# The order and engine choice of all tasks in a fused attention and GLU kernel

## The chip, the cores and the metric

The kernel runs on one core of a Trainium2 chip. The metric is the device time of one execution in microseconds (us); smaller is better. Engines are TensorE (PE in the profile), VectorE (DVE), ScalarE (ACT), GpSimd (POOL) and SyncE (SP), which here issues the DMAs.

## What is computed

One block of a conditioned transformer over 2048 tokens of width 512, with bf16 inputs and output. Cut to what matters:

```python
mod = silu(c) @ w_mod            # six vectors sa, ca, ga, sb, cb, gb of 512
h = layernorm(x) * (1 + ca) + sa
q, k, v = h @ wqkv               # 32 heads of 16
phi(t) = concat(softmax(t @ w_phi), softmax(-(t @ w_phi)))   # 32 features a head
kv = sum over tokens of phi(k) x v;   z = sum over tokens of phi(k)
o = (phi(q) @ kv) / (phi(q) @ z + 1e-6)
x = x + ga * (o @ wo)
h = layernorm(x) * (1 + cb) + sb
x = x + gb * ((sigmoid(h @ w_gate) * (h @ w_up)) @ w_down)   # inner width 1376
```

No query can be finished before kv and z hold the sum over all tokens: that is the one place where everything meets.

## The kernel before

The tokens lie in 16 tiles of 128. The kernel is written as about a thousand named tasks, each with the engines that may run it, the values that it reads and writes, and the buffers that it holds. A string, `ORDER` (lines 39 to 87), lists all of them once, in one order for all engines; a name may carry the letter of its engine (`@A` ScalarE, `@D` VectorE, `@P` GpSimd), and without one it takes its first alternative. `Graph.arrange` walks the string, gives each task its engine and hands out buffer slots (eight banks of PSUM, and fixed numbers of slots for features, reciprocals and so on), first freed, first used. `emit` then issues the tasks in that order:

```python
for word in text.split():
    name, _, e = word.partition("@")
    t = self.tasks[name]
    t.eng = LETTER[e] if e else next(iter(t.alts))
...
def emit(order):
    for t in order:
        ...
        t.fn(t.eng)
```

So every engine, and SyncE's queue of DMAs, works through its own part of the string in that order, and waits where a value or a slot is not there yet. The string sets which task stands ahead of which on an engine, and nothing else in the file does.

The tasks, by stage, with the lines under which the profile shows them:

- Head: loads of x, weights and modulation vectors (L537 to L562), `warm` (L600: 6 + 12 matmuls on zeros, whose results nobody reads), `tpw`, `wTc`, `fold`, `foldc` (L661, 664, 679, 685: w_phi folded into the projections of q and k), the modulation's matmuls `modc` (L616, 630) with their copies (L635 to 638).
- For each tile the first normalization: `st1` (statistics, VectorE, L702/703), `rs1` (ScalarE L709/710 or GpSimd L712/713), `nmr1` (L718), `xn1` (L729, 731), transposes `tph` on TensorE (L744) or by DMA, `hm1` (scale and shift: L751 on ScalarE, L753 on VectorE or GpSimd).
- Features: matmuls `K` and `Q` (L817, 871), exponentials `e`, `qe` (ScalarE, L776), sums `n`, `qn` (VectorE, L780), reciprocals `r` (VectorE L798, ScalarE L794/795), products `phi` (L787) and `qphi` (L784) on VectorE or GpSimd; values `V` (L821) and their copy `va` (L836). `phi` and `qphi` have both of their inputs in SBUF. `pT` transposes a tile's qphi by a DMA (L874).
- `kv`: the sums over all tokens (L282) in two PSUM banks; `kvn`, `kvz` (L294, 299) mask them into `kvb` on VectorE, with `mask4` (L591).
- For each tile the attention's output: `num` (L326), `rd` (L329), `u` (L333), the transposition `oT`, `out` (L356), `x1` (L361), the second normalization `st2`, `rs2`, `nmr2`, `xn2` (L365 to L400), its transposition `xnT` (L407, 415) and `mod` (scale and shift: GpSimd L424, ScalarE L426, VectorE L422).
- The GLU in six chunks of 1, 1, 2, 4, 4 and 4 tiles: for each of 11 blocks of the inner width the matmuls `g` and `u` (L447, 449, 452), `tg` (ScalarE, L457), `hm` (VectorE, L468), and for each tile 11 matmuls `y` (L485) into one accumulator; `fin` (L492) adds x1 and `st` stores.
- A guard: `bnd` (L506 to L525) bounds the exponents from the folded weights (four reductions of 1024 columns on VectorE, then small steps) and sets a flag; a second, general path behind the main one is skipped if the bound holds.

Of the kernel before, what the change touches and what calls it, by code (L numbers as in the profile page):

```python
# [43 lines left out]
modc1c1 st1_8 ld_x3a warm1_8 K1a hm1_23 xn1_5 xn1_4 tph12 nmr1_6 st1_9 hm1_03@A hm1_13@A hm1_02@A ld_wv0 wqT3 xn1_10 xn1_11 rs1_5@P K0a K0b tph31 hm1_42@A
warm1_9 hm1_12@A hm1_22@A tph32 e0.0 K3a tph30 K3b hm1_30@A ld_wmga K1b tph33 warm1_10 tph40 st1_14 st1_15 st1_13 hm1_31@A hm1_32 wqT0 e3.0 wqT1 K2b hm1_40
nmr1_5 rs1_8@P n0.0 nmr1_8 hm1_33 e2.0 V0a V1a fold03 xn1_9 xn1_8 V1b V0b e1.0 n2.0 V2a V2b tph50 hm1_50 warm1_11 xn1_15 xn1_14 n1.0 V3a wqT2 fold00 fold01
tph43 r0.0@A va1 va0 phi0.0 foldc03 fold02 foldc01 foldc02 n3.0 st1_12 foldc00 xT1_10 xT1_11 r2.0 va2@D ld_wmm2 modca.0 modca.1 hm1_60@P hm1_63@P hm1_62@P
tph82 hm1_82@A r3.0@A modcac r1.0@A phi2.0@D phi1.0@D V3b K4a K4b rs1_7@P Q0 Q2 kv0.0 Q1 qe0.0 va3 qe2.0 hm1_43@A qe1.0 modc2.0 tph52 modc2.1 tph51 nmr1_7
xn1_12 xn1_13 phi3.0@D ld_wo qn0.0 modc2c e4.0 kv1.0 qn2.0 hm1_52 kv2.0 Q4 K5a kv3.0 xT1_12 xT1_13 qphi0.0@P qphi0.1@P qn1.0 qe4.0 qphi2.1 tph80 K5b hm1_80@A
hm1_51@A e5.0 pT0 qphi2.0 n4.0 r4.0@A qn4.0 n5.0 phi4.0@D qphi1.1@P hm1_61@P qphi1.0@P tph53 V5 K7a V4 va5 hm1_53@A V6 pT2 hm1_70@P qphi4.1 va4 hm1_71 mask4  # L50
va6 K6a K7b K6b e6.0 K8 tph83 hm1_83 r5.0 qphi4.0@P e8.0 pT1 pT4 ld_wd2 tph81 hm1_81 n6.0 n8.0 e7.0 n7.0 V7 kv4.0 hm1_72@P K11 K9 V9 K14 V8 r6.0@A e9.0 va7
va9 r7.0@A e11.2 e11.6 phi5.0 phi6.0 hm1_73@P n9.0 r9.0@A kv5.0 gwa gra gwb e11.4 e14.0 K10 phi7.0@D kv6.0 K12 V10 kv7.0 e14.4 r8.0 n11.6 n11.2 r11.6 phi9.0
e10.0 e12.0 ld_wd ld_wu0 grb n11.4 n14.0 r11.2 n14.4 r14.0 n10.0 r14.4@A phi8.0 va8 V11 V14 n12.0 e11.0 K13 n11.0 phi11.6 r11.4 wo1 r11.0 va10 r10.0@A va11
kv8.0 kv9.0 phi11.2@D phi11.0@D phi10.0@D phi11.4@D V12 K15 e13.0 wmod_free ld_wg0 phi14.4 phi14.0 kv10.0 kv11.4 kv11.6 Q6 kv11.0 e13.4 r12.0@A e15.4 n13.0
n13.4 r13.0 r13.4 n15.4 e15.0 va14 V15 V13 qe6.0 va12 kv11.2 n15.0 r15.0 r15.4@A va13 phi13.4 Q5 phi15.4 phi13.0@D va15 phi15.0@D phi12.0@D wo0 wo3 Q3 kv12.0
kv13.0 kv14.0 kv15.0 qn6.0 kvn0 kvz0 kv13.4 kv14.4 kv15.4 kvz1 kvn1 num0a num1a num2a wo2 rd0a wo_all rd1a qe3.0 u0a num0b num4a num1b rd0b Q11 qe5.0 rd2a u0b
u2a rd4a num2b qn3.0 u1a rd1b tpo0 Q8 qphi6.0@P qphi6.1@P oT0 out0 num4b rd2b u1b wd0 qe11.0 u2b qphi3.1@P qphi3.0@P x1_0 rd4b st2_0 qe8.0 Q7 qe7.0 tpo1 oT1
Q10 Q9 out1 Q15 oT2 rs2_0 qn5.0 nmr2_0 xn2_0 u4a u4b x1_1 qn7.0 tsw xnT0 out2 qphi5.1@P qphi5.0@P pT6 mod02 mod00 qphi7.0@P pT3 mod03@A mod01@A qe15.0
qphi7.1@P Q13 g0.8 x1_2 tg0.8 g0.1 st2_1 wd1 rs2_1 tg0.1 u0.8 u0.1 g0.0 num3b g0.4 hm0.1 hm0.8 pT5 qe9.0 tg0.4 g0.9 wd2 u0.4 u0.9 rd3b u3b tg0.9 g0.5 num3a
hm0.4 hm0.9 u0.2 u0.0 num6a tg0.5 tg0.0 rd3a u3a u0.5 g0.2 hm0.0 hm0.5 rd6a nmr2_1 qe10.0 tg0.2 oT4 g0.10 u0.10 wd6 hm0.2 g0.3 pT7 tg0.3 u6a g0.6 num6b u0.3  # L60
y0.0 y0.1 rd6b tg0.10 hm0.10 hm0.3 num5a num5b u6b rd5b wd3 wd4 wd5 oT3 oT6 xn2_1 qe13.0 tg0.6 rd5a y0.2 u5b g0.7 tg0.7 out4 u5a oT5 qn11.0 u0.6 u0.7 xnT1
num7a hm0.6 hm0.7 mod13@A mod12@A rd7a x1_4 y0.3 out3 qphi11.1@P qphi11.0@P x1_3 st2_3 out6 mod10@A mod11@A g1.2 tg1.2 g1.1 tg1.1 num7b wd7 u1.3 u1.2 hm1.2
u7a g1.4 u1.1 y0.4 rd7b hm1.1 u1.4 y0.5 tg1.4 hm1.4 g1.0 g1.10 u1.10 g1.3 u7b st2_2 rs2_2 tg1.10 tg1.3 hm1.10 hm1.3 pT11 out5 tg1.0 u1.7 g1.7 x1_6 nmr2_2 u1.0
hm1.0 g1.5 u1.5 x1_5 qn10.0 wd8 y0.6 g1.6 oT7 xn2_2 xn2_3 g1.8 y0.7 Q14 y0.8 wd10 tg1.7 tg1.5 hm1.5 out7 u1.8 u1.6 st2_4 tg1.6 xnT2 xnT3 wd9 x1_7 qphi10.0 Q12
hm1.7 st2_6 mod21@P mod20@P qphi10.1@P y1.0 pT10 tg1.8 mod22@A mod23@A hm1.6 g1.9 y1.1 y1.2 tg1.9 u1.9 y0.9 y1.3 y1.4 g2.5 y0.10 g2.6 st2_5 qe12.0 st2_7 hm1.8
qn9.0 tg2.5 qe14.0 rs2_4 hm1.9 rs2_3 nmr2_4 y1.5 u2.0 g2.1 g2.0 tg2.0 xn2_7@D hm2.0 nmr2_3 fin0 y1.6 g2.2 tg2.2 u2.6 u2.2 hm2.2 u2.1 num11b y1.7 g2.4 rd11b
u11b xn2_6@P xnT7 xnT6 u2.5 tg2.1 xn2_5 qphi9.1@P hm2.1 tg2.6 u2.8 xn2_4 hm2.5 g2.3 num11a rd11a u11a u2.9 qphi9.0@P xnT5 y1.8 xnT4 tg2.4 u2.4 hm2.4 hm2.6
tg2.3 g2.9 u2.3 hm2.3 g2.8 tg2.8 tg2.9 u2.7 mod41@P mod43@P mod32@P mod42@P mod31@P qn13.0 g2.10 hm2.8 g2.7 y1.9 num10a qn8.0 num10b y2.0 y1.10 tg2.7 hm2.7
rd10a hm2.9 qphi8.0@P u2.10 pT9 y2.1 y2.2 y2.3 y2.4 y2.5 qn14.0 num9b rd9b qphi13.0 qphi8.1@P mod30@A mod33@A tg2.10 mod40@A y2.6 y2.7 g3.3 wr qphi13.1@P
tg3.3 oT11 g3.0 u10a rd10b u10b pT8 oT10 hm2.10 qn15.0 g3.8 num9a rd9a u9a u3.0 out11 y2.8 g3.1 y2.9 qphi14.1 fin1 x1_11 u9b u3.3 hm3.3 st1 tg3.8 tg3.0 u3.8  # L70
num8a st2_11 num8b rd8b rd8a u8a pT13 qphi15.0 hm3.8 u8b u3.9 g3.4 u3.2 out10 x1_10 qphi14.0 oT8 oT9 hm3.0 st2_10 y2.10 g3.6 u3.6 qn12.0 rs2_6 out8 tg3.4
# [987 lines left out]
```

## Time and profile before

| | before |
|---|---|
| time, median of 3 runs | 205.47 us (205.26 to 205.93) |
| span of the profiled execution | 203.3 us |
| around the span (median less span) | 2.2 us |
| TensorE busy | 194.9 us, 96% of the span, 1447 matmul records |
| VectorE busy | 160.6 us, 79% |
| ScalarE busy | 105.9 us, 52% |
| GpSimd busy | 102.1 us, 50% |
| granted TensorE clock | 9 of 9 in each slice |
| DMA | 22.94 MB, mean 113 GB/s |

The profile's own execution has no separate time beside its span; the three timed runs stand 2.2 us above it. The page cuts the span in 40 slices and gives the busy share of each engine in tenths. A group of instructions stands with its count, its busy time and the mean of one, and with the idle time of the engine just before them and what ended it. In rows of the timeline the first number is the start, the second the length, and neighbours of one kind are one row.

### The profile page before, as it was taken

Reading aid. Unit: us, or ns where it says so; the run is one execution under the profiler, and the core shown is the slowest. Engines: PE = TensorE matmul, PEld = TensorE weight load, DVE = VectorE, ACT = ScalarE, POOL = GpSimd, SP = SyncE. Lnnn points to the kernel's source line nnn. Section 1 sums busy time; section 2 is a strip of 40 time slices with the busy share of each in tenths; the row PEclk is TensorE's granted clock in tenths of the full one; section 3 lists DMA queues with packets and bytes.
Section 4 is the critical chain, followed back from the end, with each engine's and each line's share of the span. In section 5 each row is a group of like instructions: output and inputs, shape, how many; then the busy total and the mean of one; then the engine's idle time right before and its main releaser. Section 6 shows DMA issues by size and latency. Waiting matters only on the chain.

```text
span 203.3 us, 4138 instructions
## 1 busy us (share of the span) xinstructions
PE 194.9 (96%) x1447; PEld 106.7 (52%) x1471; DVE 160.6 (79%) x374; ACT 105.9 (52%) x257; POOL 102.1 (50%) x143
## 2 busy tenths in 40 slices
PE   7789999999999999999999999999999999999993
PEld 2455655555464687668844444444444444444442
DVE  3899999999999999999897797794969844326633
ACT  2799999999978984556451115212113311324100
POOL 4698977789689999767670056230030324000000
PEclk9999999999999999999999999999999999999999
DMA  5999975669952792417637224433112030100111
GB/s 172 331 329 182 233 264 102 123 82 280 400 213 43 146 102 55 94 37 106 125 59 103 51 54 103 101 83 77 26 26 69 13 79 31 40 13 7 50 55 55
DMA packets 49453, 22.94 MB, mean 113 GB/s; under 512 B 38065, under 2 KB 47634, under 8 KB 49426
## 3 DMA queue, kind: packets, MB, share of 16 engines
q1 hardware_dynamic: 48896, 22.59, 48.6%
q8 instruction: 13, 0.21, 0.4%
q14 instruction: 14, 0.11, 0.2%
q10 hardware_dynamic: 530, 0.02, 0.1%
HBM read 11.58 MB, written 2.10 MB: 67 GB/s over the span
## 4 chain that ended last, share of the span: by engine, by line
PE 75%; DVE 8%; ACT 4%; DMA 4%; issue 4%; POOL 3%; SPq 0%; POOLq 0%; DVEq 0%
PE y_ps L485 19%; PE u_ps L447 18%; PE g_ps L447 17%; PE a_ps L356 5%; DMA wmod_sb<-in_w_mod_dram 4%; PE k_ps L817 3%; PE warm L600 3%; DVE ks L780 3%; PE num L326 2%; POOL phi L787 2%; PE q_ps L871 2%; PE v_ps L821 2%; PE g_ps L449 1%; ACT h1T L751 1%; DVE qks L780 1%
## 5 line engine op out<-in xcount | busy, mean ns | idle before, releaser
L457 ACT ACTIVATE tg<-g_ps 128x512 bf16<-128x512 f32 (+5 forms) x66 | 28.8, 455 | 66.7 <-PE g_ps L447 39.5
L468 DVE SCALAR_TENSOR_TENSOR wmod_sb<-tg,u_ps 128x512 bf16<-128x512 bf16 (+4 forms) x63 | 30.3, 492 | 18.0 <-ACT tg L457 11.3
L485 PE MATMUL y_ps<-wd_sb,wmod_sb 128*128 128x512 bf16 (+4 forms) x180 | 44.2, 366 | 0.2
L447 PEld LDWEIGHTS <-wg_sb 128*128 128x128 bf16 (+1 forms) x252 | 21.9, 99 | 16.1 <-issue 0.2
L447 PEld LDWEIGHTS <-wu_sb 128*128 128x128 bf16 (+1 forms) x252 | 21.8, 99 | 16.0 <-issue 0.3
L784 POOL TENSOR_TENSOR qphi<-qe,qks 128x512 bf16<-128x512 bf16 x24 | 25.1, 1063 | 3.9 <-DMA pT<-qphi 1.0
L485 PEld LDWEIGHTS <-wmod_sb 128*128 128x128 bf16 (+1 forms) x187 | 17.1, 98 | 16.0 <-issue 0.6
L447 PE MATMUL u_ps<-wT_sb,wu_sb 128*128 128x512 bf16 (+2 forms) x124 | 23.8, 322 | 0.1
L447 PE MATMUL g_ps<-wT_sb,wg_sb 128*128 128x512 bf16 (+2 forms) x122 | 23.0, 321 | 0.2
L447 PE MATMUL g_ps<-wqk_sb,wg_sb 128*128 128x128 bf16 (+4 forms) x127 | 19.9, 286 | 0.1
L447 PE MATMUL u_ps<-wqk_sb,wu_sb 128*128 128x128 bf16 (+4 forms) x127 | 19.8, 286 | 0.2
L492 DVE TENSOR_TENSOR ot<-y_ps,x 128x512 bf16<-128x512 f32 (+2 forms) x17 | 11.1, 654 | 10.5 <-PE y_ps L485 10.4
L780 DVE TENSOR_REDUCE qks<-qe 128x64 bf16<-128x1024 bf16 x16 | 19.2, 1204 | 0.0
L780 DVE TENSOR_REDUCE ks<-e 128x64 f32<-128x1024 bf16 (+2 forms) x22 | 19.1, 905 | 0.0
L376 POOL TENSOR_SCALAR ve<-mv 128x2 f32<-128x2 f32 (+1 forms) x8 | 1.8, 226 | 34.2 <-DVE mv L366 34.1
L776 ACT ACTIVATE e<-k_ps 128x512 bf16<-128x512 f32 (+2 forms) x44 | 17.7, 504 | 0.1
L776 ACT ACTIVATE qe<-q_ps 128x512 bf16<-128x512 f32 x32 | 17.3, 608 | 0.8 <-POOL phi L787 0.4
L787 POOL TENSOR_TENSOR phi<-e,kr 128x1024 bf16<-128x1024 bf16 (+2 forms) x10 | 14.5, 1454 | 3.9 <-ACT kr L795 2.1
L817 PE MATMUL k_ps<-wqk_f,h1T 128*128 128x512 bf16 x61 | 15.9, 379 | 0.1
L356 PE MATMUL a_ps<-wo_sb,oT 128*128 128x512 bf16 x60 | 15.9, 379 | 0.2
L871 PE MATMUL q_ps<-wqk_f,h1T 128*128 128x512 bf16 x60 | 15.7, 379 | 0.2
L821 PE MATMUL v_ps<-wv_sb,h1T 128*128 128x512 bf16 x62 | 15.5, 379 | 0.0
(131 smaller groups left out, 306.4 us busy)
## 6 DMA issues: line engine op xcount, KB each, us to landing
out_dram<-ot SPq DMA_DIRECT2D x15, 128.0 KB, 1.8
x_sb<-in_A_x_dram SPq DMA_DIRECT2D x6, 256.0 KB, 4.9
wmod_sb<-in_w_mod_dram SPq DMA_DIRECT2D x1, 1536.0 KB, 7.4
wu_sb<-in_B_w_up_dram SPq DMA_DIRECT2D x1, 1376.0 KB, 11.0
wg_sb<-in_B_w_gate_dram SPq DMA_DIRECT2D x1, 1376.0 KB, 10.4
wd_sb<-in_B_w_down_dram SPq DMA_DIRECT2D x1, 1280.0 KB, 8.0
wmod_sb<-in_w_mod_dram SPq DMA_DIRECT2D x4, 256.0 KB, 6.0
wqk_sb<-in_A_wqkv_dram SPq DMA_DIRECT2D x2, 256.0 KB, 4.5
```

What stands on the lines that cost most here:

```text
L356: pe.matmul(ap_[:], lhsT=oT[:, j, :], rhs=wo_sb[:, j, :], start=(j == 0), stop=(j == KT - 1))
L447: pe.matmul(ps[:fsz, 0:n], lhsT=w[:, j, ft * P:ft * P + fsz], rhs=h[:, j, 0:n], start=(j == 0), stop=(j == KT - 1))
L457: G.add(f"tg{k}.{ft}", {"ACT": 0.13 + n * 0.00083}, lambda e, tg=tg, g_ps=g_ps, fsz=fsz, n=n: act.activation(tg[:fsz, 0:n], g_ps[:fsz, 0:n ...
L468: dve.scalar_tensor_tensor(hm_all[:fsz, hm[k].slot, ft, 0:n], tg[:fsz, 0:n], 1.0, u_ps[:fsz, 0:n], op0=ALU.add, op1=ALU.mult)
L485: mm = pe.matmul(y[:, 0:c1 - c0], lhsT=hm_all[:fsz, hm[k].slot, ft, tl * P:(tl + 1) * P], rhs=wd_sb[:fsz, ft, c0:c1], start=(ft == 0), sto ...
L776: act.activation(ee[:, a:b, s].rearrange("p g f h -> p g (f h)"), kp[:, a * 64:b * 64].rearrange("p (g n) -> p g n", n=64), ACT.Exp, scale ...
L780: dve.tensor_reduce(ks[:, a:b].rearrange("p g s h -> p (g s) h"), ee[:, a:b].rearrange("p g s f h -> p (g s) h f"), axis=AX.X, op=ALU.add)
L784: engine(e).tensor_tensor(ph[:].rearrange("p (g s f h) -> p g s f h", s=2, f=DH, h=4)[:, :, s], ee[:, :, s], ks[:, :, 1 - s].unsqueeze(2). ...
L787: engine(e).tensor_tensor(ph[:, a * P:b * P].rearrange("p (g f h) -> p g f h", f=DH, h=4), ee[:, a:b].rearrange("p g s f h -> p (g s) f h" ...
L817: pe.matmul(kp[:], lhsT=h1T[:, j, t * P:(t + 1) * P], rhs=wqk_f[:, j, D:2 * D], start=(j == 0), stop=(j == KT - 1))
L821: pe.matmul(vp[:], lhsT=h1T[:, j, t * P:(t + 1) * P], rhs=wv_sb[:, j, :], start=(j == 0), stop=(j == KT - 1))
L871: pe.matmul(qp[:], lhsT=h1T[:, j, t * P:(t + 1) * P], rhs=wqk_f[:, j, 0:D], start=(j == 0), stop=(j == KT - 1))
```

## The change

Only `ORDER` changes, nearly everywhere. The tasks are the same: 1471 matmuls, the same loads and stores. Two lines of the diff, the first of the head (the others read alike):

```diff
 ORDER = """
-pmem ld_x0b wdz warm0 c1 warm1_0 warm1_1 bd st1_2 st1_3 warm1_2 warm1_3 c2 rs1_2 ld_x0a ld_wk0 warm1_4 tpw0 st1_0 rs1_0 wTc0 st1_1 ld_wk1 rs1_1 c3 xn1_0
...
+wdz warm0 c1 c2 warm1_0 warm1_1 warm1_2 warm1_3 ld_x0a mask4 st1_1 st1_0 rs1_0 warm1_4 ld_x0b st1_2 ld_wk0 ld_wk1 ld_x1b pmem bd st1_3 rs1_2@P tpw0 tpw1 rs1_1
...
```

55 tasks get another engine. Among them: the rs1 of tile 2 (ScalarE to GpSimd); one copy of the modulation, `modc1c1` (ScalarE to VectorE, L638); h1T of tile 3, `hm1_30` (ScalarE to VectorE) and `hm1_71` (ScalarE to GpSimd); the reciprocals r2, r5 and a quarter of r11 (VectorE to ScalarE), r9 and a half each of r14 and r15 (ScalarE to VectorE); a quarter of phi11 against another; of 32 halves of qphi VectorE runs 5 rather than 8 and GpSimd 27 rather than 24; of 36 modulations `mod` GpSimd runs 12 rather than 16, ScalarE 19 rather than 16 (in part L426 for L424).

Moved, by stage: all twelve single warming matmuls stand ahead of the first K, where four stood behind it. The second part of the modulation's matmuls (L616) stands behind K6 instead of ahead of K5. The loads of wo, wd, wu and wg stand behind the first pT in SyncE's queue (before, wo's was issued at 22.0 us, the others from 40.4 to 49.3). The y accumulators of chunks 3, 4 and 5 are opened four tiles at a time, with their y between the chunk's own g and u; the guard's reductions, the qphi of tiles 8 to 15 and the modulations of the third and fourth chunk stand earlier in the string.

The first place is VectorE ahead of and around the mask (L591, `mask4`: the mask that kvb is multiplied with). Before:

```order
L780 TENSOR_REDUCE ks_760<-e_747 128x64
L787 TENSOR_TENSOR phi_762<-e_690,kr_755 128x1024
L784 TENSOR_TENSOR qphi_794<-qe_735,qks_758 128x8x64
L591 TENSOR_REDUCE mask4_77<-ident_75 128x4
L753 TENSOR_SCALAR h1T_73<-tp_h_815,modc_78 128x256
```

Now, at the very start of VectorE's work:

```order
L593 MEMSET wd_sb_71 128x256
L591 TENSOR_REDUCE mask4_77<-ident_75 128x4
L702 BN_STATS st1_81<-x_sb_65 128x6
L703 BN_AGGR mv1_82<-st1_81 128x2
```

The mask has moved from the middle of the key and query features, ahead of an h1T, to between the zeroing of the warming operand and the first statistics (st1).

The second place is TensorE around the first K (`k_ps`); `warm` are the warming matmuls, `tp_h` the transposes. Before, a row of the matmuls just behind the first K:

```order
L817 MATMUL k_ps_352<-wqk_f_67,h1T_73 128x512
L744 LDWEIGHTS xn_187
L744 MATMUL tp_h_356<-ident_75,xn_187 128x128
L600 LDWEIGHTS wd_sb_71
L600 MATMUL warm_363<-wd_sb_71 128x512
L817 LDWEIGHTS h1T_73
L817 MATMUL k_ps_365<-wqk_f_67,h1T_73 128x512
```

Now, ahead of the first modulation matmuls (L630) and of any K:

```order
L679 MATMUL fold_ps_269<-bd_101,wT_sb_99 128x128
L600 LDWEIGHTS wd_sb_71
L600 MATMUL warm_275<-wd_sb_71 128x512
L600 MATMUL warm_277<-wd_sb_71 128x512
L600 MATMUL warm_279<-wd_sb_71 128x512
L630 LDWEIGHTS wmod_sb_97
L630 MATMUL modc_ps_285<-sc_bf_106,wmod_sb_97 128x1
```

The last three warming matmuls have moved from between the K to behind the folding of w_phi (L679); their weight loads but the first are left out.

The third place is GpSimd ahead of chunk 3 of the GLU; `qphi` are halves of the query features of one tile, `wT_sb` under L424 the scaled and shifted inputs of chunk 3. Before:

```order
L398 TENSOR_SCALAR xn2_1975<-x1_1760,rs2_88,nmr_89 128x512
L784 TENSOR_TENSOR qphi_1988<-qe_1426,qks_1897 128x8x64 x2
L424 TENSOR_SCALAR wT_sb_99<-wT_sb_99,modc_78 128x256 x5
L784 TENSOR_TENSOR qphi_2099<-qe_1288,qks_2083 128x8x64 x2
L856 COPY wr_sb_72<-wg_sb_69 128x4x96
```

Now:

```order
L784 TENSOR_TENSOR qphi_1989<-qe_1552,qks_1974 128x8x64 x2
L424 TENSOR_SCALAR wT_sb_99<-wT_sb_99,modc_78 128x256
L784 TENSOR_TENSOR qphi_2044<-qe_1405,qks_2042 128x8x64 x2
L784 TENSOR_TENSOR qphi_2102<-qe_1275,qks_2077 128x8x64
L784 TENSOR_TENSOR qphi_2123<-qe_1377,qks_2109 128x8x64 x2
L424 TENSOR_SCALAR wT_sb_99<-wT_sb_99,modc_78 128x256 x3
```

Five modulations in one piece have become one, and three behind five halves of qphi.

More of the change, by code (lines that the diff above doesn't have):

```diff
@@ L44 @@
[L44 to L71, printed above, removed]
@@ L87 @@
+y13.8 y13.9 y13.10 y15.4 y15.5 st12 y14.4 y15.6 y14.5 y14.6 y14.7 fin13 y14.8 y14.9 y14.10 st13 y15.7 y15.8 fin14 st14 y15.9 y15.10 y15.0b y15.1b y15.2b
+y15.3b fin15 y15.4b y15.5b y15.6b st15 y15.7b y15.8b y15.9b y15.10b fin15b st15b
 """
```

62 lines of the change are left out of this document (44 added, 18 removed).

## The prediction

> **What bounds the kernel now.** I read the page first (busy shares, slices, chain), then the matmul timeline for the moment at which TensorE becomes dense, then the waits of TensorE and VectorE around the places where it is not.
>
> ```profile
> span 203.3 us, 4138 instructions
> PE 194.9 (96%) x1447; PEld 106.7 (52%) x1471; DVE 160.6 (79%) x374; ACT 105.9 (52%) x257; POOL 102.1 (50%) x143
> PE   7789999999999999999999999999999999999993
> DVE  3899999999999999999897797794969844326633
> PE 75%; DVE 8%; ACT 4%; DMA 4%; issue 4%; POOL 3%; SPq 0%; POOLq 0%; DVEq 0%
> ```
>
> TensorE is busy for 96% of the span, and from the fourth slice to the last but one it stands at 9. VectorE stands at 9 too, from the third slice to the nineteenth (10 to 97 us), and has room only behind that. So there are two stages: up to about 100 us two engines are full at once, and the later one of the two decides; from there on TensorE alone.
>
> ```profile
> 1.24 2.74 PE L600 MATMUL warm<-wd_sb 128*128 128x512 bf16 x6 [1.24 <-DVE wd_sb L593]
> 8.92 0.62 PE L679 MATMUL fold_ps<-bd,wT_sb 128*128 128x128 bf16 x8 [0.94 <-ACT wT_sb L664]
> 13.56 0.54 PE L630 MATMUL modc_ps<-sc_bf,wmod_sb 128*128 128x1 bf16 x16
> 14.20 0.38 PE L817 MATMUL k_ps<-wqk_f,h1T 128*128 128x512 bf16 x1
> 14.78 0.38 PE L600 MATMUL warm<-wd_sb 128*128 128x512 bf16 x1
> 58.57 0.93 PE L326 MATMUL num<-kvb,pT 128*128 128x68 bf16 x24 [0.36 <-DVE kvb L299]
> 103.41 2.75 PE L447 MATMUL g_ps<-wT_sb,wg_sb 128*128 128x512 bf16 x12
> 194.66 5.44 PE L485 MATMUL y_ps<-wd_sb,wmod_sb 128*128 128x512 bf16 x34
> ```
>
> The row at 103.41 gives the price of a 128x512 matmul in a dense row: (2.75 - 0.38) / 11 = 0.215 us. The first K comes at 14.20, and from there TensorE has only one pause worth naming, 0.36 us at 58.57: the first num (L326) waits for kvb, the masked key-value sums that VectorE makes from the last accumulation. Everything of the attention's output and of the GLU lies behind that place: 58.6 to 200.1 us, 141.5 us of TensorE, without another pause.
>
> ```profile
> 58.60:70.00 11.40, 11.15 (x97) 6.34 (x100) 11.22 (x30) 9.75 (x21) 11.24 (x12) 1.00 0.36 72
> 105.00:110.00 5.00, 4.95 (x27) 2.29 (x27) 4.30 (x9) 0.67 (x2) 1.05 (x2) 1.00 0.73 108
> 125.00:130.00 5.00, 4.95 (x39) 2.48 (x39) 2.78 (x9) 1.48 (x3) 2.59 (x4) 1.00 0.33 62
> 160.00:200.00 40.00, 39.79 (x204) 18.45 (x206) 18.65 (x42) 8.75 (x15) 4.28 (x7) 1.00 0.12 36
> ```
>
> In these rows (stretch, length, then busy time of PE, PE's loads, DVE, ACT, POOL) TensorE is full in each, VectorE in the first but not in the third and fourth. So the time of before is the time of kvb plus what TensorE has to do behind it, and the change can gain in two ways only: kvb earlier, or less TensorE work behind kvb. All 1471 matmuls stay, so the second is nothing. It can lose by a pause of TensorE anywhere behind.
>
> **The change, part by part.** Whoever brings kvb later or earlier is VectorE. Its rows up to kvb that are not work:
>
> ```profile
> DVE st L702 <- DMA x_sb<-in_A_x_dram: 2.4, 1, 2.4
> 7.94 0.46 DVE L718 TENSOR_SCALAR nmr<-mv,rs 128x1 f32<-128x1 f32 x3 [0.28 <-ACT rs L710]
> 38.02 0.28 DVE L591 TENSOR_REDUCE mask<-ident 128x4 bf16<-128x128 bf16 x1
> 38.68 0.41 DVE L753 TENSOR_SCALAR h1T<-tp_h,modc 128x256 bf16<-128x256 bf16 x1 [0.38 <-PE tp_h L744]
> DVE h1T L753 <- PE tp_h L744: 0.6, 2, 0.4
> 44.58 0.69 DVE L787 TENSOR_TENSOR phi<-e,kr 128x1024 bf16<-128x1024 bf16 x1 [0.29 <-POOL h1T L753]
> 45.19 0.55 DVE L798 RECIPROCAL kr<-ks 128x64 bf16<-128x64 f32 x1
> ```
>
> The 2.4 us for the first tokens stay: the first loads are the same size. (1) The mask (L591, 0.28 us) now runs ahead of the first statistics, in that very wait: -0.28. (2) The 0.28 us at 7.94 waits for ScalarE's rs. In the new order tile 0's normalization and the three small rows of c stand ahead of the first nmr, and tile 2's rs goes from ScalarE to GpSimd: -0.28, with 0 as the other bound. (3) The two waits of h1T for a transpose of TensorE (0.6 in all, the longer one 0.38) go if TensorE is earlier there. It is: before, four of its twelve single warming matmuls stand behind the first K (the first is the row at 14.78), now all twelve stand ahead of it, in the waits for ScalarE such as the 0.94 at 8.92. That is 4 x 0.215 = 0.86 us less ahead of 38 us, more than mask and wait together need (0.28 + 0.38 = 0.66). So -0.6, with 0 as the other bound, should ScalarE or a load hold TensorE back in their place.
>
> (4) The engine choices. Ahead of kvb VectorE gives off and takes:
>
> ```profile
> L753 DVE TENSOR_SCALAR h1T<-tp_h,modc 128x256 bf16<-128x256 bf16 x9 | 3.5, 393 | 0.6 <-PE tp_h L744 0.6
> L784 DVE TENSOR_TENSOR qphi<-qe,qks 128x512 bf16<-128x512 bf16 x8 | 3.5, 451 | 0.0
> L798 DVE RECIPROCAL kr<-ks 128x64 bf16<-128x64 f32 x3 | 1.6, 538 | 0.0
> L798 DVE RECIPROCAL kr<-ks 128x32 bf16<-128x32 f32 x4 | 1.2, 328 | 0.1
> L798 DVE RECIPROCAL kr<-ks 128x16 bf16<-128x16 f32 x4 | 0.9, 234 | 0.0
> L780 DVE TENSOR_REDUCE qks<-qe 128x64 bf16<-128x1024 bf16 x16 | 19.2, 1204 | 0.0
> ```
>
> It loses the reciprocals of tiles 2 and 5 (0.54 each) and a quarter of tile 11's (0.23), and gets that of tile 9 (0.54), a half each of tiles 14 and 15 (0.33), one h1T (0.39) and one modulation column (L638, two by two numbers a lane: no such row; between nothing and an h1T's 0.39, I take 0.2). One qks, two qphi and one quarter of phi are only exchanged for others of the same size. Net: -1.31 + 0.54 + 0.66 + 0.39 + 0.2 = +0.48. A row's end overlaps the next one's start by some 0.08 (44.58 + 0.69 against 45.19), and two more are taken than given: I take +0.3, bounds 0 and +0.5. ScalarE gets lighter by as much as that, and it was nobody's wait there except in (2). Sum at kvb: -0.28 - 0.28 - 0.6 + 0.3 = -0.86, and I take -0.8, rounded to the cautious side. TensorE's head must keep up with that: it waits 0.36 at num now, and gets 0.86 earlier by the warming matmuls, so VectorE stays the later one and the surplus is lost in the same wait.
>
> (5) K, V and Q in another order, the modulation matmuls (L616) behind K6 rather than ahead: TensorE's work up to kvb is the same, its surplus was just counted: 0. (6) The loads of wo, wg, wu, wd go behind the first transposed qphi in SyncE's queue, some 15 us later for wo. The cover is long:
>
> ```profile
> 49.99 1.17 POOL L851 TENSOR_TENSOR wo_sb<-wo_sb,ga_sb 128x512 bf16<-128x512 bf16 x1
> 49.26 0.43 SPq L559 DMA_DIRECT2D wg_sb<-in_B_w_gate_dram  x1
> wg_sb<-in_B_w_gate_dram SPq DMA_DIRECT2D x1, 1376.0 KB, 10.4
> ```
>
> The gate's weights take 10.4 us, were issued at 49.3 and are first used behind num (58.57); now they are issued some ten us earlier: 0. If the cover of wo is gone (issued at about 37 us, used by GpSimd at 50), GpSimd alone is late, on a step with the whole first GLU chunk ahead of it. (7) Behind kvb: more tiles' y accumulators are open at once, and the guard's four reductions of the folded weights, phi of queries and modulations come earlier.
>
> ```profile
> L506 DVE TENSOR_REDUCE bq<-wqk_f x4: 1207/1209/1212, 130.6 to 158.2; 128x1 f32<-128x1024 bf16 x4
> L784 POOL TENSOR_TENSOR qphi<-qe,qks 128x512 bf16<-128x512 bf16 x24 | 25.1, 1063 | 3.9 <-DMA pT<-qphi 1.0 <-DVE phi L787 0.8 <-DVE qphi L784 0.8
> L424 POOL TENSOR_SCALAR wT_sb<-wT_sb,modc 128x256 bf16<-128x256 bf16 x10 | 5.5, 562 | 5.7 <-DMA wT_sb<-xn 4.0 <-ACT tg L457 1.7
> ```
>
> The reductions (4 x 1.2 us) leave 130.6 to 158.2 us for some 120. VectorE is then full until about 134 us, where it had (row 125 to 130) 2.2 of 5 us free. TensorE's work is dense through all of it in both orders if its inputs come in time, and I count 0, which is the term with the most risk (first rival). Forecast: 205.47 - 0.8 = 204.7 us, that is a span of 202.5 beside the profiled 203.3, since 2.2 us lie around it in both. The case's own bounds: none of the waits gone but the mask, 0 - 0.28 + 0.5 = +0.2; all VectorE waits behind the first load gone (0.28 + 0.6 + 0.29), the mask, and 0 for the choices, -1.45. So 204.0 to 205.7.
>
> **The rivals.** (a) Slower: what was pulled forward makes TensorE wait in the third and fourth chunk. In the new order chunk 3's first modulation and its last three on GpSimd have five halves of qphi between them (5 x 1.063 = 5.3 us, with the three modulations 7.0), and the g of chunk 3 that needs the last one follows at about 107 us. Adding up both engines' rows from kvb on, I find it ready 0.1 to 0.6 us ahead of its use; in before the same modulations were ready 3 us ahead. The last transposed phi (tiles 13 to 15) stand 0.4 to 0.9 us ahead of their num, with VectorE full. The point at which it decides: GpSimd one qphi (1.06 us) later there than I add up. Then TensorE pauses by about half of that at each of the four places, 2.1 us in all: 204.7 + 2.1 = 206.8. For it: GpSimd waits 3.9 us ahead of its qphi in before, in pieces of up to 1.0, and now has 27 of them rather than 24. Against: its long waits there are for VectorE's statistics and leave room.
>
> (b) No gain: the waits change their place. modc's column on VectorE (4) waits for 16 matmuls of TensorE (the row at 13.56, 0.54 us) that were ScalarE's wait, and the statistics, h1T and sums of all tiles are queued behind it; the reciprocals that ScalarE took stand behind its exponentials. 0.54 there and 0.2 for the upper bound in (4) leave -0.8 + 0.74 = -0.06: 205.4 us.
>
> (c) VectorE and GpSimd shut each other out more often than now.
>
> ```profile
> 32.73 0.60 DVE L784 TENSOR_TENSOR qphi<-qe,qks 128x512 bf16<-128x512 bf16 x1
> 30.98 2.07 POOL L784 TENSOR_TENSOR qphi<-qe,qks 128x512 bf16<-128x512 bf16 x2 [0.55 <-PE kvacc L282]
> 43.99 0.56 POOL L753 TENSOR_SCALAR h1T<-h1T,modc 128x256 bf16<-128x256 bf16 x1
> L787 POOL TENSOR_TENSOR phi<-e,kr 128x1024 bf16<-128x1024 bf16 x5 | 9.6, 1917 | 1.6 <-ACT kr L795 0.9 <-PE kvacc L282 0.5
> ```
>
> A qphi of VectorE took 0.60 us rather than the mean 0.45 while GpSimd's own ran to 33.05, and VectorE's phi at 44.58 began 0.03 us after GpSimd's h1T ended (43.99 + 0.56). That is 0.15 and 0.29 us in all up to kvb: before pays little. Such instructions of VectorE are 17 after the change (20 before), but they stand at other places. Two of them behind the start of a phi of GpSimd (1.9 us each, half of it on average) ahead of kvb cost 1.9 us: 206.6. It decides from one such meeting, since the gain is 0.8. [...]
>
> **How the numbers follow.** Measurements of this kernel tell 0.3%, 0.6 us, from no change: faster is under 204.85. The forecast (204.7, own range 204.0 to 205.7) has 0.5, (a) 0.22, (b) 0.18, (c) 0.10. Faster: four fifths of the forecast's half, and little of the others, 0.43. Within 0.3%: the rest of it, most of (b), some of (a) at a fraction of its price, 0.25. Slower: most of (a) and (c), 0.32. The range reaches from 203.8 to 207.0: at the lower end the case's own bound and a little, since TensorE's surplus at kvb may be used, too; at the upper end both prices with 0.2 to spare.
>
> **What would show it.** Right: the wait of nmr for rs and those of h1T for tp_h gone from VectorE's waits; the first num at 57.8 rather than 58.57, still waiting for kvb; and the last y ending 0.8 earlier than 200.1, with TensorE at 9 in every slice between. (a) is shown by a wait of g or num (L447, L326) for GpSimd's L424 or a transposing DMA, at 105 to 125 us; (b) by the first num at 58.3 to 58.6; (c) by phi or qphi rows of VectorE above 0.7 us, or waits in front of them that end with a row of GpSimd. The forecast is wrong if the first num comes earlier by over 1.2 us or later than now, or if TensorE pauses behind it.

## The result and the profile after

The changed kernel takes 210.52 us (median of four runs, 209.93 to 210.93) where before takes 205.70 (205.26 to 206.01): the ratio is 1.0235, with a 95% interval of 1.021 to 1.026. It is slower by 4.8 us; 204.7 was forecast, with a range up to 207.0. The profiled execution has a span of 208.5 us and a time of 210.35. Around a span lie 1.7 to 1.9 us in every execution on record here; the 2.2 us in the table of before compares the median with the span of a faster execution, so that the two spans differ by 5.2 us where the medians differ by 4.8.

The page of the changed kernel, the lines that answer to those of before:

```profile
span 208.5 us, 4159 instructions
PE 196.3 (94%) x1446; PEld 107.3 (51%) x1471; DVE 162.3 (78%) x374; ACT 108.1 (52%) x256; POOL 105.2 (50%) x143
PE   7889999999859998999999999999999999999993
DVE  3789999999999997999998999965547844335252
PE 61%; DVE 14%; ACT 8%; DMA 5%; issue 5%; POOL 3%; SPq 0%; ACTq 0%; DVEq 0%
```

TensorE has a hole in the eleventh and twelfth slice (8 and 5: 52 to 63 us) and a small one in the sixteenth. From there to the last slice but one it stands at 9 as before, so the later chunks lose next to nothing. The matmul timeline shows the places, each with the wait in front of it:

```profile
54.91 0.68 PE L282 MATMUL kvacc<-vaug,phi 128*128 128x68 bf16 x16 [0.77 <-DVE phi L787]
59.95 0.81 PE L282 MATMUL kvacc<-vaug,phi 128*128 128x68 bf16 x20 [1.12 <-DVE phi L787]
61.12 0.55 PE L282 MATMUL kvacc<-vaug,phi 128*128 128x68 bf16 x12 [0.37 <-DVE phi L787]
62.66 1.05 PE L326 MATMUL num<-kvb,pT 128*128 128x68 bf16 x28 [0.99 <-DVE kvb L294]
79.79 0.39 PE L356 MATMUL a_ps<-wo_sb,oT 128*128 128x512 bf16 x1 [0.68 <-ACT tg L457]
95.08 0.20 PE L326 MATMUL num<-kvb,pT 128*128 128x68 bf16 x1 [0.44 <-DMA pT<-qphi]
```

The first num stands at 62.66, 4.1 us later than before (58.57); the other 1.1 of the span's 5.2 us come behind it, above all in the last two rows. The row at 79.79 names tg of ScalarE only because that ended last; the weight load (PEld) just ahead of it, of the oT that this matmul multiplies, waited for the transposing DMA:

```profile
79.78 0.55 PEld L356 LDWEIGHTS <-oT 128*128 128x128 bf16 x4 [0.81 <-DMA oT<-o]
```

(The granted clock of this execution is 0.999 on average; the other three have 0.988 to 0.991 and take 209.93 to 210.93, so it isn't the clock that makes this order slower.) So most of the loss is VectorE's way to kvb. Its first row under L294, in the old order and in the changed one:

```profile
57.87 0.43 DVE L294 TENSOR_TENSOR kvb<-kvacc,mask 128x256 bf16<-128x256 f32 x1
```

```profile
62.20 0.41 DVE L294 TENSOR_TENSOR kvb<-kvacc,mask 128x256 bf16<-128x256 f32 x1
```

That is 4.33 us. VectorE's own idle time on that way grew by only 0.8 us (6.05 against 5.28), by two waits at the head:

```profile
8.80 0.69 DVE L702 BATCH_NORM_STATS2 st<-x_sb 128x6 f32<-128x512 bf16 x1 [0.93 <-DMA x_sb<-in_A_x_dram]
12.11 0.21 DVE L718 TENSOR_SCALAR nmr<-mv,rs 128x1 f32<-128x1 f32 x1 [0.56 <-ACT rs L710]
```

The rest is inside its rows. Four instructions of VectorE are about three times as long as their kind; beside each stands what GpSimd (POOL) did at that time (VectorE's and GpSimd's timelines of the changed kernel):

```profile
39.68 1.28 DVE L784 TENSOR_TENSOR qphi<-qe,qks 128x512 bf16<-128x512 bf16 x1
39.40 1.27 POOL L784 TENSOR_TENSOR qphi<-qe,qks 128x512 bf16<-128x512 bf16 x1 [0.71 <-DMA pT<-qphi]
51.84 0.88 DVE L787 TENSOR_TENSOR phi<-e,kr 128x256 bf16<-128x256 bf16 x1
51.40 1.17 POOL L851 TENSOR_TENSOR wo_sb<-wo_sb,ga_sb 128x512 bf16<-128x512 bf16 x1
56.98 1.30 DVE L787 TENSOR_TENSOR phi<-e,kr 128x512 bf16<-128x512 bf16 x1
56.95 1.05 POOL L787 TENSOR_TENSOR phi<-e,kr 128x512 bf16<-128x512 bf16 x1
59.81 1.26 DVE L787 TENSOR_TENSOR phi<-e,kr 128x512 bf16<-128x512 bf16 x1
59.30 1.49 POOL L787 TENSOR_TENSOR phi<-e,kr 128x512 bf16<-128x512 bf16 x1 [1.31 <-DVE kr L798]
```

In each pair VectorE's row ends 0.15 to 0.3 us after GpSimd's; I read this as an instruction that had started and stood until GpSimd was through. For comparison, a qphi of VectorE that meets nobody (from the repaired kernel of the experiments; the one at 38.74 in the changed kernel takes as long), then the two kinds of phi before (mean ns behind the busy time):

```profile
36.55 0.41 DVE L784 TENSOR_TENSOR qphi<-qe,qks 128x512 bf16<-128x512 bf16 x1
```

```profile
L787 DVE TENSOR_TENSOR phi<-e,kr 128x256 bf16<-128x256 bf16 x3 | 0.7, 274 | 0.0
L787 DVE TENSOR_TENSOR phi<-e,kr 128x512 bf16<-128x512 bf16 x2 | 0.7, 388 | 0.0
```

By 0.41, 0.28 and 0.39 us the four rows are too long by 0.87 + 0.60 + 0.91 + 0.87 = 3.25 us. With the 0.8 of the waits that is 4.05 of the 4.33 us by which kvb is later; the engine choices are the other 0.3. This is rival (c), with four meetings in place of the two that it was priced with.

### The profile page after: what moved, and what is told of

Same layout as the page of the kernel before. It is cut to its first block, busy times and chain, and to the rows that moved or that the text cites. A ratio compares the mean times of both kernels' runs of the same rounds, so it can differ in the third digit from the quotient of the medians.

```text
span 208.5 us, 4159 instructions
## 1 busy us (share of the span) xinstructions
PE 196.3 (94%) x1446; PEld 107.3 (51%) x1471; DVE 162.3 (78%) x374; ACT 108.1 (52%) x256; POOL 105.2 (50%) x143
## 4 chain that ended last, share of the span: by engine, by line
PE 61%; DVE 14%; ACT 8%; DMA 5%; issue 5%; POOL 3%; SPq 0%; ACTq 0%; DVEq 0%
PE y_ps L485 17%; PE g_ps L447 15%; PE u_ps L447 14%; PE a_ps L356 5%; DVE ks L780 5%; PE q_ps L871 3%; ACT h1T L751 3%; DMA wqk_sb<-in_A_wqkv_dram 3%; ACT qe L776 2%; ACT e L776 2%; DVE qks L780 2%; PE num L326 2%; DMA pT<-qphi 2%; DVE phi L787 2%; PE g_ps L449 1%
## 5 line engine op out<-in xcount | busy, mean ns | idle before, releaser
L457 ACT ACTIVATE tg<-g_ps 128x512 bf16<-128x512 f32 (+2 forms) x66 | 29.4, 457 | 70.6 <-PE g_ps L447 60.3
L485 PE MATMUL y_ps<-wd_sb,wmod_sb 128*128 128x512 bf16 (+3 forms) x179 | 44.2, 366 | 0.3
L784 POOL TENSOR_TENSOR qphi<-qe,qks 128x512 bf16<-128x512 bf16 x27 | 28.8, 1088 | 8.9 <-DVE qks L780 7.4
L787 POOL TENSOR_TENSOR phi<-e,kr 128x1024 bf16<-128x1024 bf16 (+2 forms) x10 | 15.0, 1509 | 5.4 <-DVE kr L798 2.6
L821 PE MATMUL v_ps<-wv_sb,h1T 128*128 128x512 bf16 x62 | 16.1, 379 | 0.2
L871 PE MATMUL q_ps<-wqk_f,h1T 128*128 128x512 bf16 x62 | 15.2, 379 | 0.1
```

What stands on the lines that cost most here:

```text
L457: G.add(f"tg{k}.{ft}", {"ACT": 0.13 + n * 0.00083}, lambda e, tg=tg, g_ps=g_ps, fsz=fsz, n=n: act.activation(tg[:fsz, 0:n], g_ps[:fsz, 0:n ...
L485: mm = pe.matmul(y[:, 0:c1 - c0], lhsT=hm_all[:fsz, hm[k].slot, ft, tl * P:(tl + 1) * P], rhs=wd_sb[:fsz, ft, c0:c1], start=(ft == 0), sto ...
L784: engine(e).tensor_tensor(ph[:].rearrange("p (g s f h) -> p g s f h", s=2, f=DH, h=4)[:, :, s], ee[:, :, s], ks[:, :, 1 - s].unsqueeze(2). ...
L787: engine(e).tensor_tensor(ph[:, a * P:b * P].rearrange("p (g f h) -> p g f h", f=DH, h=4), ee[:, a:b].rearrange("p g s f h -> p (g s) f h" ...
L821: pe.matmul(vp[:], lhsT=h1T[:, j, t * P:(t + 1) * P], rhs=wv_sb[:, j, :], start=(j == 0), stop=(j == KT - 1))
L871: pe.matmul(qp[:], lhsT=h1T[:, j, t * P:(t + 1) * P], rhs=wqk_f[:, j, 0:D], start=(j == 0), stop=(j == KT - 1))
```

## The experiments

All times below are medians; the old order ran beside each of them, at 205.3 to 205.7 us. The theory: VectorE's two-input instructions and GpSimd's shut each other out, and this costs what VectorE's rows show. The rival: the long rows only fill slack, and the time goes to the amount or the order of work, ahead of kvb or behind.

**Head and tail apart.** First kernel: the new order up to the last kvn, and the old order of all that remains. Second: the old order up to there, and the new one behind. Only `ORDER` is cut and joined.

> The new order up to the second kvn, and behind it all remaining tasks in the old order. If the time is lost ahead of kvb (VectorE and GpSimd shut each other out at four places, 3.2 us, and VectorE's head waits 0.8 us longer): the first num at about 62.6 us as in the new order, time 205.7 + 4.1 = 209.8 us, between 209.3 and 210.3. If it is lost behind kvb, by what the new order pulls forward: first num at 58 to 59 us, time 205 to 206.5.

> The old order up to the second kvn, and behind it all remaining tasks in the new order. If the time is lost ahead of kvb: first num at 58.6 us, time 205.7, plus at most the 1.1 us of two waits for transposing DMAs (oT at 79.8, pT at 95.1 in the new order): 205.5 to 206.9. If it is lost behind kvb: 209 to 210.5.

The new head gave 210.87 us (ratio 1.0234, 1.018 to 1.029), the new tail 207.54 (1.0106, 1.004 to 1.017), both above the ranges that I gave them. The first num of both (matmul timelines, new head first):

```profile
60.96 1.52 PE L326 MATMUL num<-kvb,pT 128*128 128x68 bf16 x24 [0.98 <-DVE kvb L294]
```

```profile
58.37 1.05 PE L326 MATMUL num<-kvb,pT 128*128 128x68 bf16 x28 [0.36 <-DVE kvb L299]
```

The head is enough to lose 2.4 us by num (60.96 against 58.57). The other 3.6 us of its span (209.3 against 203.3) come behind. Two things are seen in this execution: the same 24 num take 1.52 us where before has 0.93, at a granted clock of 0.61 and 0.53 (last column but two), right behind TensorE's waits for phi and kvb; and there is a pause shortly behind the place where the two orders are joined (windows, then TensorE's timeline).

```profile
60.00:62.00 2.00, 1.04 (x19) 1.04 (x19) 2.00 (x6) 0.82 (x2) 2.00 (x3) 0.61 0.00 0
62.00:64.00 2.00, 1.78 (x15) 0.93 (x14) 2.00 (x9) 0.00 (x0) 2.00 (x3) 0.53 0.00 0
```

```profile
58.23 0.81 PE L282 MATMUL kvacc<-vaug,phi 128*128 128x68 bf16 x20 [1.12 <-DVE phi L787]
...
70.49 1.04 PE L356 MATMUL a_ps<-wo_sb,oT 128*128 128x512 bf16 x4 [1.38 <-ACT oT L347]
```

By the clock, up to 2 x 0.39 + 2 x 0.47 = 1.7 us at full rate are missing (TensorE had work for 1.04 and 1.78 us of the two stretches), and the pause is 1.4. But three further executions had a mean clock of 1.00 and took 210.48 to 211.29 all the same, so the total doesn't hang on the clock; what stands in its place there was not profiled, and stays open. The new tail on the old head loses 1.9 us by itself. Both parts are slower, then, the head by more; the two don't add up, since 5.2 and 1.9 us are more than the 4.8 of the whole change, and each seems to lose something at the joint. The new head also shows what the waits at 8.80 and 12.11 were: they aren't there in this execution, nor is TensorE's wait of 0.91 us for a load of wqk, behind whose copies ScalarE's rs stood. The loads landed at other times in the one execution than in the other.

**One meeting made.** In the old order GpSimd is idle from 55.25 to 56.48 us. One multiply of wo is put there:

```diff
-... va13 phi13.4 Q5 phi15.4 phi13.0@D va15 phi15.0@D phi12.0@D wo0 wo3 Q3
+... va13 phi13.4 wo0 Q5 phi15.4 phi13.0@D va15 phi15.0@D phi12.0@D wo3 Q3
```

> The old order with one GpSimd instruction moved into GpSimd's own idle time: the multiply wo0 (1.16 us, two inputs in SBUF) stands ahead of the last quarter of phi rather than behind it, and so runs from 55.25 us on, where VectorE is about to start its phi of tile 13. Nobody waits for wo0 before 68 us. If the two engines exclude each other: VectorE's phi of tile 13 ends at 56.4 or later rather than at 55.84 (its row 0.9 to 1.3 us rather than 0.36), kvb comes 0.6 to 1.0 us later, time 206.3 to 206.7. If they don't, and the long rows of the new order have another cause: no change, 205.7.

It took 209.74 us (208.00 to 210.75), ratio 1.0184 (1.013 to 1.024): 4.1 us for one instruction moved into idle time, far more than either theory said. VectorE's timeline, then GpSimd's:

```profile
55.90 3.93 DVE L787 TENSOR_TENSOR phi<-e,kr 128x512 bf16<-128x512 bf16 x3
```

```profile
55.63 1.16 POOL L851 TENSOR_TENSOR wo_sb<-wo_sb,ga_sb 128x512 bf16<-128x512 bf16 x1
56.89 1.09 POOL L787 TENSOR_TENSOR phi<-e,kr 128x512 bf16<-128x512 bf16 x1
57.94 2.92 POOL L851 TENSOR_TENSOR wo_sb<-wo_sb,ga_sb 128x512 bf16<-128x512 bf16 x2
```

Three phi of VectorE stand in one row of 3.93 us, where the next experiment shows 1.29. The rows read as if they were held up not once but three times: GpSimd's instructions of 1.16, 1.09 and 1.46 us (half of the row of two) follow each other with at most 0.10 us between them, one for each of VectorE's three. That is 2.6 of the 3.0 us by which the first num is later in the profiled execution (61.57 against 58.57), which was the fastest of the six. The others go roughly with the clock that TensorE was granted: 208.00, 208.26 and 209.59 us at a mean of 0.990 to 0.992, 209.89 at 0.984, 210.46 and 210.75 at 0.975 and 0.976. So of the 4.1 us up to two may go with a lower clock and not with the meetings; where in those executions it fell, wasn't profiled.

**The same place, without reading.** Two memsets of GpSimd at that place, into a buffer that nobody reads, the order otherwise as before:

```diff
+    zz = cst.tile([P, 1024], BF16, name="zz")
+    def f_zz(e):
+        for i in range(2):
+            pool.memset(zz[:, 512 * i:512 * i + 512], 0.0)
-... va13 phi13.4 Q5 phi15.4
+... va13 phi13.4 zz Q5 phi15.4
```

> The old order, with two extra memsets on GpSimd of 512 bf16 numbers a lane into a buffer that nobody reads, at the place where the moved wo0 stood in the experiment before (from 55.25 us on, ahead of VectorE's phi of tile 13). They write SBUF and read nothing. If any instruction of GpSimd that touches SBUF shuts VectorE out, or if the cause is an order between the engines rather than the memory: VectorE's phi of tile 13 takes as long as the memsets need, time over 206.3 us. If only a GpSimd instruction that reads SBUF does so: phi of tile 13 stays at 0.36 to 0.42 us and the time at 205.7, at most 0.4 us more where the last quarter of phi on GpSimd is pushed back.

205.27 us, ratio 0.9979 (0.995 to 1.001): nothing.

```profile
54.84 0.99 POOL L597 MEMSET zz<- 128x512 bf16 x2
```

```profile
55.12 1.29 DVE L793 TENSOR_TENSOR phi<-e,kr 128x512 bf16<-128x512 bf16 x3
```

GpSimd worked from 54.84 to 55.83 over the start of the three phi (under L793 here, as the added lines move the file on by six), and they took 1.29 us. So GpSimd being busy and writing is not enough, nor is an order that the program sets between the engines; the memsets differ from the multiply, with which the three phi took 3.93 us, in that they read nothing.

**Meetings taken out of the new order.** Two halves of phi go from GpSimd to VectorE, and GpSimd's four multiplies of wo are left out:

```diff
-phi13.4 ... phi15.4
+phi13.4@D ... phi15.4@D
-    ... engine(e).tensor_tensor(wo_sb[:, j, :], wo_sb[:, j, :], ga_sb[:], op=ALU.mult),
+    ... None,
```

> The new order, with the last halves of phi of tiles 13 and 15 given to VectorE, which is full there, and the four multiplies of wo by the gate left out (GpSimd idles instead; the output lacks that gate). VectorE gets two instructions more (0.39 each, +0.7 us by starts). If the meetings with GpSimd's instructions are what cost, three of four are gone (51.84, 56.98, 59.81: 0.6 + 0.9 + 0.9 us): kvb 1.7 us earlier than in the new order, first num at 61.0, time about 208.9. If VectorE's amount of work is what counts: kvb 0.7 us later, first num at 63.4, time 211.2.

207.72 us, 2.8 less than the changed kernel, with more work on the full engine. VectorE's timeline at the place:

```profile
55.25 0.74 DVE L787 TENSOR_TENSOR phi<-e,kr 128x512 bf16<-128x512 bf16 x2
56.98 1.29 DVE L787 TENSOR_TENSOR phi<-e,kr 128x1024 bf16<-128x1024 bf16 x3
59.40 0.42 DVE L294 TENSOR_TENSOR kvb<-kvacc,mask 128x256 bf16<-128x256 f32 x1
```

kvb comes at 59.40, against 62.20 in the changed kernel and 60.49 in the kernel with the new head. Part of that is luck: the waits at the head are missing in this execution as in that of the new head. The stretch behind them is free of that: from the 128x256 phi (51.84 in the changed kernel, 50.13 and 50.78 in the other two) to kvb it is 10.36 us in the changed kernel and with the new head, and 8.62 here. The 1.74 us are what was expected, 1.7: three meetings less, two instructions more. VectorE's amount of work falls as the cause. Of the time's 2.8 us the rest can't be put down to the meetings; GpSimd's lighter queue and the loads are in it.

**Repair with nothing left out.** The same two halves of phi on VectorE, the half of qphi of 39.68 on GpSimd, three multiplies of wo behind the first query features after kvb, and the two late places of the tail put later:

```diff
-phi13.4 ... phi15.4 ... qphi0.1 ... wo3 ... wo2 ... wo0 kvn0 qphi5.1@P
+phi13.4@D ... phi15.4@D ... qphi0.1@P ... kvn0 qphi5.1@P wo3 wo2 wo0
```

> The new order, repaired, nothing left out: the last halves of phi of tiles 13 and 15 on VectorE, the query feature half that met GpSimd at 39.7 us on GpSimd, three multiplies of wo behind the first query features after kvb, and the two late places of the tail put later as above. If the meetings of VectorE and GpSimd are the cause ahead of kvb (three of four are gone, 2.6 us, for 0.4 us of work): first num at 58 to 59 us in place of 61 to 62.7, time 205 to 206.5. If they only filled slack: first num at 61 or later, time 209.5 or more.

208.85 us, ratio to the old order 1.016 (1.011 to 1.021): 1.7 us won back, not four. The first num comes at 59.62, short of the 58 to 59 expected. One of the four meetings is left (a multiply of wo beside VectorE's 128x256 phi), and two new waits eat of the gain (VectorE's timeline, then TensorE's row of the waits):

```profile
42.93 1.22 DVE L780 TENSOR_REDUCE ks<-e 128x64 f32<-128x1024 bf16 x1 [0.96 <-ACT e L776]
```

```profile
PE a_ps L356 <- POOL wo_sb L851: 0.9, 1, 0.9
```

With VectorE faster, ScalarE's exponentials are late by 0.96; and wo, moved away from VectorE's phi, is now late for the first out. The rest of the distance to the old order was not followed up.

**The tail.** On the old head with the new tail, out of tile 2 and some num of tiles 8 and 11 were put later, first by about one us, then by more and with x1 of tile 2 too:

```diff
-out2 wd2 xn2_1 ... x1_2 ... pT8 num8a num8b ... pT11 num11b ... u2.1
+... y0.1 out2 y0.2 x1_2 ... pT8 ... pT11 num11b ... u2.0 num8a num8b
+... y0.2 out2 ... hm0.6 x1_2 ... pT8 ... pT11 ... u2.1 num8a num8b num11b
```

> The old order up to kvb and the new order behind (as in the run that gave 207.5), with two places of the new order put later: out of tile 2 with its x1 behind two of the next y (0.9 us later), and the first two num of tile 8 behind the first u of chunk 2 (1.2 us later). If the new tail costs by those two waits for transposing DMAs: 0.7 to 1.3 us less, 206.3 to 206.9. If it costs by VectorE's or GpSimd's work that was pulled forward: no change, 207.5.

> The old order up to kvb and the new order behind it, with the same two places as in the last attempt put later by more, and on both engines: out of tile 2 behind three y of chunk 0, its x1 on VectorE two tasks further (it held VectorE for 1.17 us in the last attempt), and the num of tiles 8 and 11 behind the second u of chunk 2. If the new tail costs by VectorE standing in its own queue behind an input that a transposing DMA brings late: 1 to 1.6 us less than the 207.3 to 207.5 of the unmended tail, 205.8 to 206.5. If by the amount of work that VectorE and GpSimd got earlier: 207 or more.

The first gave 207.28 us, the second 206.82, from 207.54. In the first, TensorE's wait went over to VectorE, which stood in its queue behind x1 (VectorE's timeline):

```profile
78.62 0.69 DVE L361 TENSOR_TENSOR x<-a_ps,x_sb 128x512 f32<-128x512 f32 x1 [1.17 <-PE a_ps L356]
```

The profile of the unmended tail has both waits for transposing DMAs (0.44 us for oT, 0.57 for pT). By the medians the late transposes are 0.7 us of its 1.9, but the intervals (1.004 to 1.017, and 1.001 to 1.008 for the second repair) overlap, and both times lie between those expected for the two causes: the size isn't shown. Of the rest, short of a test, waits of 0.2 and 0.3 us stand where the two orders were joined; what remains stays open.

**Parts of the change alone, on the old order.** First the mask at the start and all warming matmuls ahead of the first K:

```diff
-wdz warm0 ... tph00 fold11 fold13 ... fold12 ... warm1_8 K1a ... mask4
+wdz mask4 warm0 ... tph00 warm1_5 warm1_6 fold11 fold13 warm1_7 ... fold12 warm1_8 ... K1a
```

> The old order with two parts of the change alone: the mask runs in VectorE's first wait, and seven of the single warming matmuls stand earlier, all twelve ahead of the first K, four of them in TensorE's waits for the folding. The prediction's terms (1) and (3): -0.28 and -0.6, first num at 57.7, time 204.9. If VectorE's shift against GpSimd makes a new meeting ahead of kvb: first num at 58.6 or later and a row of phi or qphi of VectorE over 0.5 us, time 205.7 or more.

205.51 us, ratio 0.999 (0.996 to 1.003), from 203.91 to 207.66. The profiled execution (206.97) shows a wait of 2.17 us, which the old order's profile doesn't have, in front of a qphi of VectorE. What leads to it stands on TensorE (VectorE's timeline, TensorE's, and the windows):

```profile
34.56 0.76 DVE L784 TENSOR_TENSOR qphi<-qe,qks 128x512 bf16<-128x512 bf16 x2 [2.17 <-PE kvacc L282]
```

```profile
29.08 0.83 PE L616 MATMUL modc_ps<-sc_bf,wmod_sb 128*128 128x1 bf16 x24 [0.70 <-DMA wmod_sb<-in_w_mod_dram]
31.51 1.90 PE L871 MATMUL q_ps<-wqk_f,h1T 128*128 128x512 bf16 x4
```

```profile
28.00:30.00 2.00, 1.30 (x33) 0.93 (x32) 2.00 (x4) 2.00 (x6) 1.50 (x2) 1.00 0.55 185
30.00:32.00 2.00, 2.00 (x45) 1.73 (x43) 2.00 (x3) 1.90 (x7) 0.74 (x2) 0.69 0.72 72
32.00:34.00 2.00, 2.00 (x6) 0.69 (x5) 0.40 (x1) 0.57 (x3) 1.41 (x2) 0.50 0.37 68
34.00:36.00 2.00, 2.00 (x20) 1.21 (x19) 1.44 (x3) 1.86 (x5) 0.53 (x1) 0.96 0.68 131
```

The matmuls of the modulation's second part (L616), which this order reaches earlier, wait 0.70 us for their weights (0.22 in the old order's profile); right behind them the granted clock (last column but two) falls to 0.69 and 0.50, and four Q matmuls take 1.90 us where 0.215 each is the dense rate. The sums over the tokens (L282) that end VectorE's wait stand behind those matmuls in TensorE's queue, and so come late. So L616 was put behind K6 as the new order has it; beside it the same with rs1 of tile 2 on GpSimd and c's rows behind tile 0's normalization; and then L616 four tasks later:

```diff
-qe1.0 modc2.0 tph52 modc2.1 ... K6b e6.0 K8 tph83 ... tph81
+qe1.0 tph52 ... K6b modc2.0 modc2.1 modc2c e6.0 K8 tph83 ... tph81
+qe1.0 tph52 ... K6b e6.0 K8 tph83 ... tph81 modc2.0 modc2.1 modc2c
```

> The old order with the mask in VectorE's first wait, all warming matmuls ahead of the first K, and the second part of the modulation's matmuls (L616) behind K6 as in the new order. In the run without that last part TensorE waited for their weights, by an amount that differs from run to run. If that wait was what ate the gain: 204.4 to 204.9 and less spread. If the gain is lost to meetings of VectorE and GpSimd or to other waits ahead of kvb: 205.3 or more.

> As the run beside it, with the prediction's term (2) too: rs1 of tile 2 on GpSimd and the three small rows of c behind tile 0's normalization. If term (2) holds: 0.2 to 0.3 us less than the run beside it. If not: the same, or a new meeting.

> As the run with mask, warming matmuls and L616 moved (204.97 us), with L616 put four tasks later, behind the last two transposes of tile pair 8 instead of ahead of them: in that run VectorE waited 1.16 us at 38.4 us for one of these transposes, which stood behind the 1.5 us of L616 in TensorE's queue. If VectorE's chain to kvb still sets the time, as the prediction's first part has it: 0.5 to 1.1 us less, 203.9 to 204.5, first num at 57.2 to 57.8. If TensorE's own work up to kvb, or a meeting of VectorE and GpSimd that the shift makes, sets it now: 204.8 or more.

They took 204.97 us (ratio 0.9943, 0.991 to 0.997), 205.36 (0.996, 0.993 to 0.999) and 205.03 (0.998, 0.997 to 0.999; one of its twelve executions took 1147 us, for a reason that stays open). So term (2), added in the second, won nothing: nmr still waits 0.21 us for rs there, which it doesn't in the first. The first and the third show why not more comes of it (VectorE's timelines):

```profile
38.44 0.41 DVE L753 TENSOR_SCALAR h1T<-tp_h,modc 128x256 bf16<-128x256 bf16 x1 [1.16 <-PE tp_h L744]
```

```profile
42.98 1.22 DVE L780 TENSOR_REDUCE ks<-e 128x64 f32<-128x1024 bf16 x1 [0.95 <-ACT e L776]
44.81 0.69 DVE L787 TENSOR_TENSOR phi<-e,kr 128x1024 bf16<-128x1024 bf16 x1 [0.60 <-POOL h1T L753]
```

Whatever VectorE saves early it waits for later: for TensorE's transposes while L616 stands ahead of them, and when that is mended, for ScalarE's exponentials, and then for a GpSimd instruction. The best of these is about half a per cent faster than the old order. It is also steadier: its twelve executions have a clock of 0.997 to 1.000 and take 204.63 to 205.64 us. Against the six executions of the old order beside it that had the full clock (median 205.39) it wins 0.4 us rather than 0.65.

## Why the prediction was wrong

- What bounds the kernel: right. kvb sets the time of all behind it, and the 4.1 us of the head went to the end unchanged, with TensorE dense behind 95 us.
- Terms (1) to (3), VectorE's waits: right in part. In the kernel with the new head the waits for rs and for h1T's transposes are gone. Its kvb came at 60.49, 2.62 later than before, with four long rows that are too long by 3.25 us in all (by the same reckoning as above), so that everything else is worth about -0.6, where the sum said -0.8. But in the changed kernel's own profile nmr waits 0.56 us for rs, twice as long as before, and VectorE is idle 0.8 us more rather than 1.16 less: the sum gave the loads at the head no spread. On the old order (1) and (3) with L616 moved brought kvb only from 57.87 to 57.62, where they were priced at 0.88: the rest was waited for again, for TensorE's transposes or for ScalarE's exponentials, though the prediction had called ScalarE nobody's wait. Adding (2) brought it back to 58.13.
- Term (4), the engine choices: right as VectorE's work. VectorE is busy for 3.56 us more up to kvb, 3.25 of them the meetings, and 0.31 is left where the sum took 0.3.
- The step that failed is what stands in none of the terms and has a chance of 0.10 under (c): that VectorE's two-input instructions meet GpSimd's. The sum has nothing for them, and the rival counts such instructions (17 for 20), which was the wrong measure. The two rows of before, 0.15 and 0.29 us, were read as the price of a meeting; they are what is left where an order avoids meetings. What avoided them stands in GpSimd's timeline of before:

```profile
52.19 3.06 POOL L787 TENSOR_TENSOR phi<-e,kr 128x512 bf16<-128x512 bf16 x3 [1.03 <-DVE phi L787]
56.48 1.20 POOL L787 TENSOR_TENSOR phi<-e,kr 128x512 bf16<-128x512 bf16 x1 [1.23 <-ACT kr L795]
```

Its three phi ended at 55.25, its fourth waited until 56.48 for a reciprocal of ScalarE, and in that gap VectorE's three phi went through at 0.43 each (VectorE's timeline of before):

```profile
55.47 1.29 DVE L787 TENSOR_TENSOR phi<-e,kr 128x512 bf16<-128x512 bf16 x3
```

In the new order GpSimd's three begin 2.74 us later and VectorE's phi only 1.51 later, so the third of GpSimd's (56.95) falls on VectorE's (56.98); and the reciprocal is VectorE's own, right behind which both engines start a phi (59.30 and 59.81). That reciprocal is one of the engine choices that (4) priced as 0.33 us of VectorE's time and nothing else.
- The price under (c), two meetings at half of a phi of 1.9 us, was an estimate that no row of before shows: the two there are 0.15 and 0.29 us. It was of the right size for each (0.60 to 0.91 in the changed kernel) and wrong in number: four, 3.25 us.
- Terms (5) and (6) at nothing: no wait for these loads shows. wo was issued at 43.34 rather than the 37 reckoned with, and its first multiply began at 51.40, right behind GpSimd's phi.
- Term (7) at nothing: wrong by 1.1 us in the changed kernel. Rival (a) had the mechanism partly (num behind a late pT) but the wrong chunk: the waits are at 79.8 and 95.1, and between 105 and 125 us, where it looked, TensorE stands at 9: GpSimd's last modulation for chunk 3 ended at 111.72, and the first g of that chunk began at 112.50.
- Rival (b): modc's column waits 0.25 us for its matmuls in the changed kernel; it made no difference beside the rest.
- The range ended at 207.0 since (a) and (c) were taken as alternatives. They came together; but at the prices that they were given, both would have made 204.7 + 2.1 + 1.9 = 208.7 us, so the number of meetings and the idle time at the head were wrong besides.
